# Attention and two expert layers on one core: two heads' products on halves of the TensorE array, and a scale taken from x1 itself

## The chip, the core and the metric

The kernel runs on one core of a Trainium2 chip, in one launch. The metric is the device time of that launch in microseconds (us); the kernel before takes 1054.92 us, the median of three runs (1052.87 to 1056.31).

## The reference, cut to what matters

Three stages follow one another. First an attention over 2 batches of 8 heads, 576 positions, 64 wide, which adds two results: a global one on positions averaged in fours, and a local one in which a position sees only neighbours less than 4 away.

```python
q_d, k_d, v_d = (a.reshape(B, H, 144, 4, 64).mean(axis=3) for a in (q, k, v))
out_up = np.repeat(sm_attn(q_d, k_d, v_d), 4, axis=2)       # softmax(q k^T / 8) v
mask = np.abs(pos[:, None] - pos[None, :]) < 4
attn = softmax(np.where(mask, q @ k^T / 8, -1e9))
x1 = out_up + attn @ v                                      # -> [1152 tokens, 512]
act = silu(x1 @ w_gate) * (x1 @ w_val)                      # 512 -> 1536
x2 = act @ w_out                                            # 1536 -> 512
P = eight rounds of row and column normalising of exp(x2 @ w_gate2)
out = sum over 8 experts e of P[:, e] * (relu(x2 @ w1[e]) @ w2[e])   # 512 -> 1024 -> 512
```

## The kernel before, in words

**Attention** (`attention`, lines 332 to 480). The 16 heads are worked as 8 pairs; a pair's two heads of 64 lie on the 128 partitions, the first on partitions 0 to 63. `load_pair` (287) loads k of a pair as one transfer and q as two, each head into its own half of a zeroed tile `qz` (288 KB in all for q): column block j holds head j on its 64 partitions and zeros on the others. So the product of `qz` block j with the whole k tile is head j's score, contracted over all 128 rows of the array. `scores(h)` (360) writes one head: a mask product, five windows of 128x128 positions (lines 366 to 372), and two products of the pooled q and k (line 374), into two of six PSUM banks (`bank`, tag "att"). VectorE takes the maxima, ScalarE the exponentials with their sums, GpSimd divides by the sums. `turn(h)` (404) transposes the weights on TensorE and ScalarE copies them back, again through two of the six banks. `combine(pr)` (421) multiplies them with v: `vz` and `vdz` hold v of each head beside 64 zero columns, so that the two heads' products, each 128 columns of weights wide, accumulate in the same PSUM columns (lines 430 and 438, 8 and 20 matmul instructions a pair, each f32 product being two). The result x1 of a pair, 128 features by 576 tokens, is scaled and split into two f16 parts `xhl` at once (line 450).

**Order of the pieces.** Each generator step is one piece in program order: the scores of 4 heads ahead (`AHEAD`), then turn(h), scores(h+4), and after each odd h combine. Tile pools hand out buffers, and a planner that follows program order as priority and its own cost model sets the order on each engine; that order is fixed in the program. All loads go through SP's one queue in program order: two `load_pair`, two `load_v` (two transfers for `vz`, one for `v4` each), then `load_va`, eight loads of a copy of v, 288 KB each, in four buffers. The next pair's loads wait for the buffers of the pair two back.

**The scale of x1.** x1 is bounded ahead of the attention from v: `x1_scale` (314) multiplies v by itself on TensorE (40 bf16 matmuls, line 322), takes the largest entry and makes a power of two of it (`pow2`), one for all of x1. The loads of `va` serve this alone.

**After it.** `gv_step` multiplies `xhl` with the gate and value weights, chunk 0 (tokens 0 to 511) in 24 matmuls of 512 columns for each of 12 weight tiles f, chunk 1 (tokens 512 to 1151) in 48 of 320, three f later (`LAG`). The first three f of chunk 0 (`NX`) use PSUM left over beside the attention, the others banks that the attention gives back at its end. The weights come as 64-bit floats: `prep_gv` (200) and `prep_wo` (214) convert, scale and split them, mostly on VectorE and ScalarE, in f order; two are placed in the attention's program (`PREP_AT`), others run beside it where there is room. From about 270 us on the two-layer experts follow, with no part in the change.

Of the kernel before, what the change touches and what calls it, by code (L numbers as in the profile page):

```python
# [7 lines left out]
F32 = mybir.dt.float32  # L8
# [31 lines left out]
AHEAD = 4  # L40
# [15 lines left out]
def tile_kernel(ctx, tc, qT, kT, vw, vd4, va, wgv, wo, wg2, w1, w2, out):  # L56
# [25 lines left out]
    qz = [ap.tile([P, 2, S], F32, tag=f"qz{i}", bufs=1, name=f"qz{i}") for i in range(2)]  # L82
    vz = [ap.tile([P, NW, 2, P], F32, tag=f"vz{i}", bufs=1, name=f"vz{i}") for i in range(2)]
    vdz = [ap.tile([HS, 2, 2, P], F32, tag=f"vdz{i}", bufs=1, name=f"vdz{i}") for i in range(2)]
# [12 lines left out]
    for i in range(2):  # L97
        G.memset(vz[i][:, :, 0, 64:], 0.0)
        G.memset(vz[i][:, :, 1, :64], 0.0)
        G.memset(vdz[i][:, :, 0, 64:], 0.0)  # L100
        G.memset(vdz[i][:, :, 1, :64], 0.0)
# [185 lines left out]
    def load_pair(pr):  # L287
        k = ap.tile([P, S], F32, tag="k", name=f"k{pr}")
        nc.sync.dma_start(k, kT[pr])
        q = qz[pr % 2]  # L290
        nc.sync.dma_start(q[:64, 0], qT[pr, :64])
        nc.sync.dma_start(q[64:, 1], qT[pr, 64:])
        ld[pr] = k

    v4s = {}

    def load_v(pr):
        v = vz[pr % 2]
        for j in range(2):
            nc.sync.dma_start(v[:, :, j, 64 * j:64 * j + 64], vw[pr, :, :, 64 * j:64 * j + 64])  # L300
        v4 = ap.tile([HS, 2, FAC, P], F32, tag="v4", bufs=1, name=f"v4{pr}")
        nc.sync.dma_start(v4, vd4[pr])
        v4s[pr] = v4

    vas = []
    x1s = []

    def load_va():
        for i in range(B * NPAIR):
            t = mp.tile([P, 2 * CH[1][1]], F32, tag="xT", bufs=4, name=f"va{i}")[:, :S]  # L310
            nc.sync.dma_start(t, va[i])
            vas.append(t)

    def x1_scale():


        ps = psg.tile([P, 512], F32, tag="y", name="vv")[:, :P]
        for i, t in enumerate(vas):
            b = t.bitcast(BF16)[:, 1::2]
            for lo in (0, P, 2 * P, 4 * P, 3 * P):  # L320
                n = min(P, S - lo)
                T.matmul(ps[:n, :n], lhsT=b[:, lo:lo + n], rhs=b[:, lo:lo + n],
                         start=(i, lo) == (0, 0), stop=(i, lo) == (B * NPAIR - 1, 3 * P))
        mx = tmp(1, "mxv")
        V.tensor_reduce(mx, ps, axis=AX.X, op=ALU.max)
        m = tmp(1, "mv")
        V.tensor_scalar(m.bitcast(U32), allmax(mx, 1, "v", True).bitcast(U32), 0x7F800000, 1, op0=ALU.bitwise_and,
                        op1=ALU.logical_shift_right)
        V.tensor_scalar(m.bitcast(U32), m.bitcast(U32), float(127 << 22), None, op0=ALU.add)
        x1s.extend(pow2(m, 1, "x1", room=4.0))  # L330

    def attention():
# [4 lines left out]
        qd, kd, exs, ats = {}, {}, {}, {}  # L337

        def pooled(pr):
            q, k = qz[pr % 2], ld[pr]  # L340
            qd[pr] = ap.tile([P, 2, SD], F32, tag="qd", name=f"qd{pr}")
            kd[pr] = ap.tile([P, SD], F32, tag="kd", name=f"kd{pr}")
            V.tensor_reduce(kd[pr], k.rearrange("p (s a) -> p s a", a=FAC), axis=AX.X, op=ALU.add)
            if pr not in QDV:
                t = ap.tile([P, 2, 2 * SD], F32, tag="qt", bufs=1, name=f"qt{pr}")
                G.tensor_tensor(t, q[:, :, 0::2], q[:, :, 1::2], op=ALU.add)
                G.tensor_tensor(qd[pr], t[:, :, 0::2], t[:, :, 1::2], op=ALU.add)
            else:
                V.tensor_reduce(qd[pr], q.rearrange("p j (s a) -> p j s a", a=FAC), axis=AX.X, op=ALU.add)

        def pooled_v(pr):
            v4, vd = v4s[pr], vdz[pr % 2]
            vt = ap.tile([HS, 2, 2, P], F32, tag="vt", bufs=1, name=f"vt{pr}")
            G.tensor_tensor(vt[:, 0], v4[:, :, 0], v4[:, :, 1], op=ALU.add)
            G.tensor_tensor(vt[:, 1], v4[:, :, 2], v4[:, :, 3], op=ALU.add)
            for j in range(2):
                h = slice(64 * j, 64 * j + 64)
                G.tensor_tensor(vd[:, :, j, h], vt[:, 0, :, h], vt[:, 1, :, h], op=ALU.add)

        def scores(h):  # L360
            pr, j = h // 2, h % 2
            q, k = qz[pr % 2], ld[pr]
            nm = f"{h}"
            ps = bank(f"s{nm}")
            T.matmul(ps[0], lhsT=identb, rhs=maskb.rearrange("p u w -> p (u w)"), start=True, stop=False)
            for w in range(NW - 1):
                ws = slice(WSTART[w], WSTART[w] + P)
                T.matmul(ps[0][:, w * P:(w + 1) * P], lhsT=q[:, j, ws], rhs=k[:, ws],  # L368
                         start=False, stop=w == NW - 2)
            T.matmul(ps[1][:, DW:DW + P], lhsT=identb, rhs=maskb[:, 0], start=True, stop=False)  # L370
            ws = slice(WSTART[4], WSTART[4] + P)
            T.matmul(ps[1][:, DW:DW + P], lhsT=q[:, j, ws], rhs=k[:, ws], start=False, stop=True)
            for t in range(2):
                T.matmul(ps[1][:HS, t * SD:(t + 1) * SD], lhsT=qd[pr][:, j, t * HS:(t + 1) * HS],
                         rhs=kd[pr], start=True, stop=True)
# [45 lines left out]
        def combine(pr):  # L421
            nm = f"{pr}"
            v, vd = vz[pr % 2], vdz[pr % 2]
            ps = bank(f"o{nm}")
            base = WCUT[3]
            nr = S - base
            n = 0
            for j in range(2):
                for c in range(2):
                    T.matmul(ps[1][:, nr:nr + SD], lhsT=vd[:, c, j], rhs=ats[2 * pr + j][:HS, 1, c * SD:(c + 1) * SD],  # L430
                             start=n == 0, stop=n == 3)
                    n += 1
            for w in range(NW):
                lo, hi = WCUT[w], WCUT[w + 1]
                dst = ps[0][:, lo:hi] if w < 3 else ps[1][:, lo - base:hi - base]
                off = (w * P if w < 4 else DW) + lo - WSTART[w]
                for j in range(2):
# [10 lines left out]
            b, k = pr // NPAIR, pr % NPAIR  # L448
            o = slice(b * S, (b + 1) * S)
            split(xhl[:, 0, k, o], xhl[:, 1, k, o], x1, x1s[0])  # L450

        NH = 2 * NPAIR * B

        def start(h):
            if h < NH:
                if h % 2 == 0:
                    pooled(h // 2)
                scores(h)
                if h % 2 and h // 2 + 2 < NPAIR * B:
                    load_pair(h // 2 + 2)  # L460

        for h in range(AHEAD):
            start(h)
            if h == 1:
                pooled_v(0)
                x1_scale()
            yield
        for h in range(NH):
            turn(h)
            yield  # L470
            start(h + AHEAD)
            yield
            if h % 2:
                pr = h // 2
                combine(pr)
                if pr + 2 < NPAIR * B:
                    load_v(pr + 2)
                if pr + 1 < NPAIR * B:
                    pooled_v(pr + 1)
# [7 lines left out]
    def gv_step(c, f, early):  # L487
# [4 lines left out]
        with tc.high_priority():  # L492
            V.tensor_scalar(iv[:, 0:1], gv_inv[f], x1s[1], 0.5 if early else 1.0, op0=ALU.mult, op1=ALU.mult)
# [138 lines left out]
    load_va()  # L632
# [150 lines left out]
_INS = ("qT", "kT", "vw", "vd4", "va", "wgv", "wo", "wg2", "w1", "w2")  # L783
# [38 lines left out]
```

## Time and profile before

| what | value |
|---|---|
| median of the runs | 1054.92 us (1052.87 to 1056.31) |
| the profiled execution | 1055.02 us, span 1053.2 us |
| TensorE (PE) busy | 1019.6 us, 97% |
| VectorE (DVE) busy | 767.7 us, 73% |
| ScalarE (ACT) busy | 450.1 us, 43% |
| GpSimd (POOL) busy | 94.3 us, 9% |
| read from HBM | 64.50 MB |

All later times are counted in the span of the profiled execution; 1.8 us lie around it. PE stands for TensorE's matmuls and PEld for its weight loads, which overlap them; SPq is SyncE's queue, which issues the transfers. L368 is line 368 of the kernel. An f32 product appears as two matmul instructions. The duration that a row gives for one matmul runs to the modelled end of its pipeline; the pace of a row of matmuls is read from the chain of waits, which gives starts. "PEclk" is the clock that was granted to TensorE, 1.00 being 2.4 GHz and 0.5 the lower level of 1.2 GHz; values between are mixtures over a stretch.

### The profile page before, as it was taken

To read this page: it belongs to the slowest core of one execution; us is meant where nothing else is said; L and a number is where in the kernel's file an instruction comes from. 1 tells how busy PE (TensorE), PEld (TensorE's weight loads), DVE (VectorE), ACT (ScalarE), POOL (GpSimd) and SP (SyncE) were. 2 spreads that over 40 slices of the span, in tenths; PEclk is the share of its full clock that TensorE was granted. 3 is DMA by queue.
4 is the path that set the end of the run, shared out by engine and by line. 5 is a ranking of instruction groups with operands and counts; after the bars stand their busy time and mean duration, and the time that the engine had idled before them with its cause. 6 is when DMAs were issued, how large, how long until landed. Compare 5 with 4: busy or idle time off the path is not lost.

```text
span 1053.2 us, 16460 instructions
## 1 busy us (share of the span) xinstructions
PE 1019.6 (97%) x6520; PEld 655.2 (62%) x6521; DVE 767.7 (73%) x1578; ACT 450.1 (43%) x931; POOL 94.3 (9%) x138
## 2 busy tenths in 40 slices
PE   6787998999999999999999999999999999999998
PEld 4676754656567866665756756666575675666644
DVE  7888559887681899878759749758875974984631
ACT  3586656756460656345215414414521541441200
POOL 4786100000000200000000000000000000000000
PEclk9899899999999999999999999999999999999999
DMA  9652132432020022112112100301211110020011
GB/s 263 189 146 52 56 118 85 156 121 81 1 81 1 2 81 80 42 40 81 41 40 79 43 16 26 120 1 41 80 41 40 76 46 17 24 81 1 1 41 51
DMA packets 23614, 67.93 MB, mean 64 GB/s; under 512 B 12208, under 2 KB 12464, under 8 KB 17136
## 3 DMA queue, kind: packets, MB, share of 16 engines
q1 hardware_dynamic: 23536, 66.87, 19.1%
q8 instruction: 51, 0.84, 0.3%
q14 instruction: 27, 0.22, 0.1%
HBM read 64.50 MB, written 2.36 MB: 63 GB/s over the span
## 4 chain that ended last, share of the span: by engine, by line
PE 86%; DVE 6%; ACT 3%; DMA 2%; issue 2%; SPq 0%; POOL 0%; ACTq 0%; DVEq 0%
PE y L172 35%; PE p L172 30%; PE gv L172 8%; PE wo L172 7%; DMA k<-in_kT 2%; PE o L438 2%; ACT ex L386 1%; PE o L430 1%; DVE cvg L196 1%; PE s L368 1%; PE lgps L556 1%; DVE cvg L191 1%; DVE cvg L195 0%; PE t L410 0%; DVE act L528 0%
## 5 line engine op out<-in xcount | busy, mean ns | idle before, releaser
L172 PE MATMUL y<-w,hhl 128*128 128x512 f16 (+1 forms) x1752 | 396.2, 376 | 0.0
L172 PE MATMUL p<-bop,w 128*128 128x320 f16 (+1 forms) x2688 | 354.6, 286 | 0.8 <-DVE u L693 0.7
L172 PEld LDWEIGHTS <-w 128*128 128x128 f16 x2688 | 263.0, 98 | 90.8 <-issue 1.5
L172 PEld LDWEIGHTS <-hhl 128*128 128x128 f16 x1752 | 171.4, 98 | 178.2
L721 ACT ACTIVATE hhl<-h 128x640 f16<-128x640 f32 (+1 forms) x128 | 83.3, 676 | 160.6 <-DVE h L693 160.5
L172 PE MATMUL gv<-xhl,gv 128*128 128x320 f16 (+1 forms) x864 | 145.5, 328 | 6.5 <-ACT gv L164 4.1
L172 PEld LDWEIGHTS <-gv 128*128 128x128 f16 x864 | 84.2, 98 | 62.8 <-issue 5.6
L752 DVE SCALAR_TENSOR_TENSOR acc<-y,pe,acc 128x512 f32<-128x512 f32 (+1 forms) x64 | 47.3, 740 | 101.3 <-PE y L172 100.5
L164 ACT ACTIVATE w<-r,s_w 128x256 f16<-128x256 f32 (+1 forms) x96 | 71.1, 783 | 115.2 <-PE y L172 86.3
L722 DVE SCALAR_TENSOR_TENSOR hhl<-h,hhl 128x640 f16<-128x640 f32 (+1 forms) x128 | 94.6, 754 | 15.2 <-ACT hhl L721 13.7
L693 DVE SCALAR_TENSOR_TENSOR h<-p,u 128x256 f32<-128x256 f32 (+1 forms) x192 | 85.2, 453 | 19.9 <-PE p L172 14.0
L165 DVE SCALAR_TENSOR_TENSOR w<-r,s_w,w 128x256 f16<-128x256 f32 (+1 forms) x96 | 78.2, 834 | 16.8 <-ACT w L164 16.7
L172 PE MATMUL wo<-ahl,wo 128*128 128x320 f16 (+1 forms) x432 | 71.5, 326 | 0.0
L693 DVE SCALAR_TENSOR_TENSOR u<-p,u 128x320 f32<-128x320 f32 (+1 forms) x128 | 57.5, 449 | 4.3 <-PE p L172 3.2
L164 ACT ACTIVATE w<-cmb,s_w 128x512 f16<-128x512 f32 x64 | 43.0, 710 | 40.5 <-DVE cmb L253 37.9
L172 PEld LDWEIGHTS <-wo 128*128 128x128 f16 x432 | 42.3, 99 | 26.9
L151 POOL PARTITION_ALL_REDUCE g_w<-gm_w x16 | 5.9, 372 | 569.1 <-DVE gm_w L147 563.2
L710 ACT ACTIVATE s<-p 128x256 f32<-128x256 f32 (+1 forms) x64 | 25.4, 397 | 56.5 <-PE p L172 56.4
L141 DVE TENSOR_REDUCE mxw<-r 128x1 f32<-128x1024 f32 x32 | 37.5, 1213 | 12.6 <-DMA r<-in_w 12.6
L165 DVE SCALAR_TENSOR_TENSOR w<-cmb,s_w,w 128x512 f16<-128x512 f32 x64 | 46.2, 743 | 0.0
L273 ACT ACTIVATE j<-r 128x1024 f16<-128x1024 f32 x32 | 33.4, 1045 | 26.0 <-DMA r<-in_w 26.0
L693 DVE SCALAR_TENSOR_TENSOR u<-p,s 128x256 f32<-128x256 f32 (+1 forms) x64 | 28.8, 451 | 5.2 <-PE p L172 3.9
(201 smaller groups left out, 952.4 us busy)
## 6 DMA issues: line engine op xcount, KB each, us to landing
r<-in_w SPq DMA_DIRECT2D x32, 1024.0 KB, 5.4
rawg<-in_wgv SPq DMA_DIRECT2D x12, 1024.0 KB, 6.4
rawo<-in_wo SPq DMA_DIRECT2D x6, 1024.0 KB, 4.8
vz<-in_vw SPq DMA_DIRECT2D x16, 160.0 KB, 3.4
k<-in_kT SPq DMA_DIRECT2D x8, 288.0 KB, 6.5
qz<-in_qT SPq DMA_DIRECT2D x16, 144.0 KB, 4.4
v<-in_vd SPq DMA_DIRECT2D x8, 288.0 KB
va<-in_va SPq DMA_DIRECT2D x8, 288.0 KB, 7.7
```

The lines of the kernel that those rows point to most:

```text
L141: V.tensor_reduce(o, i, axis=axis, op=ALU.max, apply_absolute_value=True)
L164: return (A.activation(hi, src, AF.Copy, scale=s), V.scalar_tensor_tensor(lo, src, s, hi, op0=ALU.mult, op1=ALU.subtract))
L165: V.scalar_tensor_tensor(lo, src, s, hi, op0=ALU.mult, op1=ALU.subtract))
L172: T.matmul(ps, lhsT=wf(i, k), rhs=xf(j, k), start=n == 0, stop=n == 3 * nk - 1)
L191: V.scalar_tensor_tensor(f, h, HI_MIN, f, op0=ALU.max, op1=ALU.max)
L273: A.activation(junk, t[:, 2 * j:2 * j + 2].rearrange("p a n -> p (a n)"), AF.Abs, accum_out=mx[:, 2 * i + j:2 * i + j + 1])
L438: T.matmul(dst, lhsT=v[:, w, j], rhs=ats[2 * pr + j][:, w // 4, off:off + hi - lo], start=j == 0, stop=j == 1)
L693: V.scalar_tensor_tensor(o, ps, HSC, u, op0=ALU.mult, op1=ALU.add)
L710: A.activation(s1, p1, AF.Copy, scale=HSC)
L721: ra = A.activation(t[:, 0], h, AF.Relu)
L722: rv = V.scalar_tensor_tensor(t[:, 1], h, 0.0, t[:, 0], op0=ALU.max, op1=ALU.subtract)
L752: V.scalar_tensor_tensor(acc[t][:, ds], ps, p[:, t:t + 1], acc[t][:, ds], op0=ALU.mult, op1=ALU.add)
```

## The change

q, v and the pooled forms are kept without zeros, one tile with a head on each half. A score product uses the 64 partitions of its head for both operands, and the two heads' products of a pair are issued alternately; in `combine` each head uses 64 columns of weights and writes its own 64 PSUM partitions, alternately as well. The scores of a pair are one piece now, into four of the six banks. q, and v, come as one transfer each. The zero fills, `load_va` and `x1_scale` are gone; instead the magnitudes of each x1 are taken, and the splitting waits for the last pair of a batch: `x1_split(0)` splits the first 512 tokens by the largest of pairs 0 to 3 and copies the last 64 aside, `x1_split(1)` splits the rest by the largest of all eight. `gv_step` uses the inverse scale of its chunk.

```diff
-    for i in range(2):
-        G.memset(qz[i][64:, 0], 0.0)
-        G.memset(qz[i][:64, 1], 0.0)
...
-        q = qz[pr % 2]
-        nc.sync.dma_start(q[:64, 0], qT[pr, :64])
-        nc.sync.dma_start(q[64:, 1], qT[pr, 64:])
+        q = ap.tile([P, S], F32, tag="q", name=f"q{pr}")
+        nc.sync.dma_start(q, qT[pr])
...
+        v_s[pr] = ap.tile([P, NW, P], F32, tag="v", name=f"v{pr}")
+        nc.sync.dma_start(v_s[pr], vw[pr])
...
-    def x1_scale():
-        ps = psg.tile([P, 512], F32, tag="y", name="vv")[:, :P]
-        for i, t in enumerate(vas):
...
+    def x1_split(b, x1):
+        mx = x1mx[:, :(b + 1) * NPAIR]
+        s, x1i[b] = pow2(allmax(mx, (b + 1) * NPAIR, f"x1{b}", True), 1, f"x1{b}")
+        n = CH[1][0] if b == 0 else S
+        if b:
+            o = slice(CH[1][0], S)
+            split(xhl[:, 0, :, o], xhl[:, 1, :, o], tail, s)
+        for k, t in enumerate(x1):
+            o = slice(b * S, b * S + n)
+            split(xhl[:, 0, k, o], xhl[:, 1, k, o], t[:, :n], s)
+            if b == 0:
+                A.copy(tail[:, k], t[:, n:])
...
+        def scores(pr):
+            q, k = ld[pr]
+            pss = [bank(f"s{2 * pr + j}") for j in range(2)]
+            hj = [slice(64 * j, 64 * j + 64) for j in range(2)]
...
+            for w in range(NW):
+                ws = slice(WSTART[w], WSTART[w] + P)
+                for ps, h in zip(pss, hj):
+                    dst = ps[0][:, w * P:(w + 1) * P] if w < 4 else ps[1][:, DW:DW + P]
+                    T.matmul(dst, lhsT=q[h, ws], rhs=k[h, ws], start=False, stop=w >= NW - 2)
+            for t in range(2):
+                for ps, h in zip(pss, hj):
+                    T.matmul(ps[1][:HS, t * SD:(t + 1) * SD], lhsT=qd[pr][h, t * HS:(t + 1) * HS],
+                             rhs=kd[pr][h], start=True, stop=True)
             for j in range(2):
+                weights(2 * pr + j, pss[j])
...
+            for c in range(2):
+                for j, h in enumerate(hj):
+                    T.matmul(ps[1][h, nr:nr + SD], lhsT=vd[:, c, h], rhs=ats[2 * pr + j][:HS, 1, c * SD:(c + 1) * SD],
+                             start=c == 0, stop=c == 1)
...
-                    T.matmul(dst, lhsT=v[:, w, j], rhs=ats[2 * pr + j][:, w // 4, off:off + hi - lo],
-                             start=j == 0, stop=j == 1)
+                for j, h in enumerate(hj):
+                    T.matmul(dst[h], lhsT=v[:, w, h], rhs=ats[2 * pr + j][:, w // 4, off:off + hi - lo],
+                             start=True, stop=True)
...
-            split(xhl[:, 0, k, o], xhl[:, 1, k, o], x1, x1s[0])
+            absmax(x1mx[:, pr:pr + 1], x1)
+            x1t.append(x1)
+            if len(x1t) == NPAIR:
+                x1_split(pr // NPAIR, x1t)
+                x1t.clear()
...
+        for pr in range(2):
+            start(pr)
...
+        for pr in range(NP):
+            for h in (2 * pr, 2 * pr + 1):
+                turn(h)
+                yield
+            start(pr + 2)
             yield
+            combine(pr)
```

## Rows read from the trace of the kernel before

**Rows 1.** From the page: busy time, share of the span and instructions of each engine.
```profile
PE 1019.6 (97%) x6520; PEld 655.2 (62%) x6521; DVE 767.7 (73%) x1578; ACT 450.1 (43%) x931; POOL 94.3 (9%) x138
```

**Rows 2.** Busy time by stretch (start:end, length, busy us and instructions of each engine, granted clock, busy share of the DMA engines, GB/s): up to the first x1, the rest of the attention, the gate-and-value stage in two parts, and the experts.
```profile
0.00:47.00 47.00, 31.38 (x200) 26.14 (x202) 36.94 (x90) 22.23 (x97) 27.26 (x45) 0.89 0.86 242
47.00:129.00 82.00, 73.77 (x547) 63.63 (x546) 62.05 (x146) 59.25 (x216) 49.37 (x63) 0.94 0.32 87
129.00:180.00 51.00, 45.54 (x255) 24.71 (x254) 37.16 (x69) 28.91 (x46) 0.73 (x2) 0.97 0.28 104
180.00:270.00 90.00, 89.82 (x577) 56.36 (x576) 73.49 (x134) 58.93 (x106) 3.23 (x6) 1.00 0.30 106
...
400.00:1053.00 653.00, 649.92 (x4057) 396.81 (x4055) 460.67 (x923) 220.47 (x372) 4.55 (x13) 1.00 0.13 46
```

**Rows 3.** VectorE on the timeline, the x1 of a pair: the first of the eight and the last (start, duration of both instructions).
```profile
46.97 0.81 DVE L444 TENSOR_TENSOR x<-o,avd 128x364 f32<-128x364 f32 x2
...
128.61 0.82 DVE L444 TENSOR_TENSOR x<-o,avd 128x364 f32<-128x364 f32 x2
```

**Rows 4.** The chain of work that ended last, in order of time (start, us, what), from 16 to 47 us.
```profile
16.54 9.17 DMA k<-in_kT
25.77 9.62 DMA k<-in_kT
...
35.56 0.52 issue
36.09 1.15 DVE nb L380
...
38.89 1.33 PE o L430 x4
40.22 0.51 PE sm_v L157 x2
40.73 2.85 PE o L438 x12
43.58 0.97 PE o L430 x4
44.55 1.65 PE o L438 x8
```

**Rows 5.** The DMA view of the first 40 us: packets and bytes, and the queue's share of the 16 engines' time.
```profile
DMA packets 6185, 10.29 MB, mean 257 GB/s; under 512 B 3225, under 2 KB 3225, under 8 KB 5798
...
q1 hardware_dynamic: 6182, 10.26, 93.2%
```

**Rows 6.** The line that loads k, over the whole run: its transfers' time from issue to landing.
```profile
DMA to landing us min/median/max: 3.1/6.5/9.6
```

**Rows 7.** The timeline of the first 11 us: what VectorE does ahead of the identity matrix, and TensorE's first scores behind it.
```profile
1.24 3.77 DVE L109 TENSOR_SCALAR dist<-dist 128x1 f32<-128x1 f32 x5
...
5.69 1.35 DVE L349 TENSOR_REDUCE qd<-qz 128x288 f32<-128x1152 f32 x1
...
7.65 0.75 DVE L343 TENSOR_REDUCE kd<-k 128x144 f32<-128x576 f32 x1
...
10.09 0.23 DVE L117 TENSOR_SCALAR identb<-dist 128x128 bf16<-128x128 f32 x1
...
10.71 0.59 PE L365 MATMUL s<-maskb,identb 128*128 128x512 bf16 x1 [7.22 <-DMA vz<-in_vw]
```

**Rows 8.** The chain again, at the full clock, from which the pace of each kind of matmul is read (us for xcount of them, one head or one pair).
```profile
71.06 0.25 PE t L414 x4
71.31 0.22 PE s L365
71.53 0.89 PE s L368 x8
72.48 0.28 PE s L372 x2
72.75 0.49 PE s L374 x4
73.24 0.44 PE t L410 x4
...
80.23 0.49 PE o L430 x4
80.72 0.86 PE o L438 x8
...
127.26 5.18 PE gv L172 x24
```

**Rows 9.** TensorE's first products of v with itself on the timeline (start, duration of all).
```profile
16.84 2.11 PE L322 MATMUL vv<-va 128*128 128x128 bf16 x20
```

**Rows 10.** Groups by line and form over 0 to 135 us (busy us, mean ns of one, idle before): the score matmuls, and the weight loads of the products of v with itself.
```profile
L368 PE MATMUL s<-k,qz 128*128 128x128 f32 x128 | 18.1, 286 | 0.7 <-DMA k<-in_kT 0.6
...
L322 PEld LDWEIGHTS <-va 128*128 128x128 bf16 x32 | 2.3, 98 | 1.0 <-DMA va<-in_va 0.6
```

**Rows 11.** Whom TensorE waited for in the first 130 us (us in total, times, longest).
```profile
PE o L430 <- ACT ex L386: 9.5, 3, 4.7
```

**Rows 12.** ScalarE on the timeline, one head's exponentials from the first to the copies behind the last.
```profile
63.06 0.37 ACT L386 ACTIVATE ex<-s,nb 128x128 f32<-128x128 f32 x1 [0.31 <-DVE nb L383]
...
65.49 0.59 ACT L416 COPY at<-t 128x512 f32<-128x512 f32 x1
```

**Rows 13.** Busy time in stretches of 10 us (columns as in rows 2): where the granted clock fell.
```profile
30.00:40.00 10.00, 5.11 (x37) 3.97 (x36) 7.90 (x18) 3.84 (x19) 5.34 (x6) 0.80 0.90 237
40.00:50.00 10.00, 10.00 (x62) 9.45 (x62) 9.27 (x21) 6.49 (x27) 10.00 (x14) 0.69 0.47 148
```

More of the change, by code (lines that the diff above doesn't have):

```diff
@@ L95, in tile_kernel @@
         V.memset(sts[i], 1.0)
[L97 to L101, printed above, removed]
+    x1mx = cp.tile([P, B * NPAIR], F32, name="x1mx")
+    tail = ap.tile([P, KD, S - CH[1][0]], F32, tag="tail", bufs=1, name="tail")
     ones = cp.tile([P, P], F32, name="ones")
@@ L305, in tile_kernel @@
[L305 to L312, printed above, removed]
-    def x1_scale():
-        ps = psg.tile([P, 512], F32, tag="y", name="vv")[:, :P]
-        for i, t in enumerate(vas):
[L319 to L330, printed above, removed]
+        q = ap.tile([P, S], F32, tag="q", name=f"q{pr}")
@@ L355, in pooled_v @@
             G.tensor_tensor(vt[:, 1], v4[:, :, 2], v4[:, :, 3], op=ALU.add)
-            for j in range(2):
[L357 to L362, printed above, removed]
-            nm = f"{h}"
[L364 to L375, printed above, removed]
+            G.tensor_tensor(vds[pr], vt[:, 0], vt[:, 1], op=ALU.add)
@@ new lines, in scores @@
+        def scores(pr):
+            q, k = ld[pr]
+            pss = [bank(f"s{2 * pr + j}") for j in range(2)]
+            hj = [slice(64 * j, 64 * j + 64) for j in range(2)]
+            for ps in pss:
+                T.matmul(ps[0], lhsT=identb, rhs=maskb.rearrange("p u w -> p (u w)"), start=True, stop=False)
+            for ps in pss:
+                T.matmul(ps[1][:, DW:DW + P], lhsT=identb, rhs=maskb[:, 0], start=True, stop=False)
+            for w in range(NW):
[7 more added lines that the diff above has]
+                             rhs=kd[pr][h], start=True, stop=True)
+            for j in range(2):
+                weights(2 * pr + j, pss[j])
@@ L376, in scores, with weights @@
+        def weights(h, ps):
+            nm = f"{h}"
             mx, sm = stm[h % 2], sts[h % 2]
@@ L426, in combine @@
             nr = S - base
[L427 to L432, printed above, removed]
+            hj = [slice(64 * j, 64 * j + 64) for j in range(2)]
+            for c in range(2):
+                for j, h in enumerate(hj):
+                    T.matmul(ps[1][h, nr:nr + SD], lhsT=vd[:, c, h], rhs=ats[2 * pr + j][:HS, 1, c * SD:(c + 1) * SD],
+                             start=c == 0, stop=c == 1)
             for w in range(NW):
@@ L447, in combine, with start @@
                                 op=ALU.add)
-            b, k = pr // NPAIR, pr % NPAIR
-            o = slice(b * S, (b + 1) * S)
-            split(xhl[:, 0, k, o], xhl[:, 1, k, o], x1, x1s[0])
[L452 to L464, printed above, removed]
+            absmax(x1mx[:, pr:pr + 1], x1)
[3 more added lines that the diff above has]
+                x1t.clear()
+        NP = NPAIR * B
+        def start(pr):
+            if pr < NP:
+                pooled(pr)
+                scores(pr)
+                if pr + 2 < NP:
+                    load_pair(pr + 2)
+        for pr in range(2):
+            start(pr)
+            if pr == 0:
                 pooled_v(0)
-                x1_scale()
             yield
-        for h in range(NH):
-            turn(h)
             yield
-            start(h + AHEAD)
-            yield
[L473 to L479, printed above, removed]
+        for pr in range(NP):
[3 more added lines that the diff above has]
+            start(pr + 2)
+            yield
+            combine(pr)
+            if pr + 2 < NP:
+                load_v(pr + 2)
+            if pr + 1 < NP:
+                pooled_v(pr + 1)
+            yield
+            yield
             yield
```

45 lines of the change are left out of this document (18 added, 27 removed).

## The prediction

> **What bounds the kernel now.** I read the page first: TensorE is busy for 97% of the span [rows 1], so whatever does not give TensorE less work, or less waiting, gives nothing. The table by stretch says where waiting is left [rows 2]: from 180 us on there is none (89.8 of 90 us, 649.9 of 653), up to 47 us there are 15.6 us of it, in the rest of the attention 8.2, and up to 180 us 5.5. The change touches the attention, so it can win in the first 129 us and must hand on what it wins to the gate-and-value stage, which is in step with TensorE only as long as its weights are converted in time.
>
> The eight x1 give the pace of the attention [rows 3]: the first at 46.97, the last at 128.61, so 11.66 us a pair behind a long start. The chain of waits explains the start [rows 4]: from 16.5 to 35.4 it is nothing but two loads of k, 9.17 and 9.62 us each, then VectorE, then the first combine at 38.9, which had waited for its bank [rows 11]. These loads are late because the queue is full: in the first 40 us the transfers take 93.2% of the 16 engines' time for 10.26 MB, 257 GB/s [rows 5], while the quickest load of k landed in 3.1 us [rows 6]. In the second part, from 47 to 129 us, TensorE is the tightest engine, 73.8 of 82 us; VectorE has 62.1, ScalarE 59.3, GpSimd 49.4 [rows 2].
>
> **The change, part by part.**
>
> *Loads.* `load_va` took 8 x 288 KB = 2.36 MB out of the one queue, all issued before 24 us: at 257 GB/s [rows 5] 9.2 us of a queue on which the chain waits for 18.8 us [rows 4]. Each of the two loads of k stands behind about half of it, so I expect them to land in about 4.6 and 5.0 us. Merging the halves of q and of v takes SP issues away, two a pair, of which none stands in the chain behind 16 us; I put it at nothing. Bounds: 9.2 us if the chain ends at the queue, 0 if VectorE (36.9 of 47 us busy) takes its place. I take 8, nearer to the chain's row than to VectorE's, because that engine idles for 10 us here. Behind the loads VectorE's maxima are late next.
>
> *VectorE at the start.* The identity matrix, for which the first score really waits (it is written at 10.09, the score starts at 10.71), stands in VectorE's queue behind two reductions of `qz` over 1152 columns, 1.35 us each; over 576 one takes 0.75 [rows 7]. That is 1.2 us. The five small operations that take 3.77 us beside GpSimd's zero fills [rows 7] may lose some 2 us as those go; I count 0 and keep the 2 as a bound. Together the first pair comes about 9 us earlier (0 to 13).
>
> *TensorE's work per pair.* At the full clock one head's scores take 0.22 for the mask, 0.89 and 0.28 for ten window matmuls, 0.06 for the small mask between them, 0.49 for the pooled ones; one turn 0.44 + 0.11 + 0.25; a combine 2 x 0.49 + 20 x 0.1075 = 3.1 [rows 8]. A pair is 2 x 1.94 + 2 x 0.80 + 3.1 = 8.6 us. On two halves the pooled products fall from 0.98 to 0.49 and the combine from 3.1 to 1.6, if the halves run beside each other. The windows (2.34 a pair) are open between no gain and half: the products of v with itself, 128 columns of weights against 128 moving columns in bf16, come every 2.11 / 20 = 0.105 us [rows 9], though 512 moving columns take 0.216 (5.18 / 24) [rows 8] and so 128 about 0.054; their loads take 98 ns each [rows 10]. So a load of 128 columns paces its matmul, and the windows keep 128 columns of weights for each head. The combine has 64 and escapes this. By this row the windows stay at 2.34, and a pair costs 0.56 + 2.34 + 0.49 + 1.6 + 1.6 = 6.6 us; if the loads of the two halves overlapped, the windows would take 1.17 and a pair 5.4. I take 6.6, as the row has it. The Trainium skill says in TensorEngine Tiling (Key Properties) that different tiles load weights and multiply in parallel, which would be the 5.4; no row of this kernel shows two tiles at work. Either way 2.0 to 3.2 us a pair go, 16 to 26 in all, and `x1_scale` takes 40 x 0.105 = 4.2 with it. The sum hardly hangs on which, since TensorE is not the tightest engine then.
>
> *What is late next.* Without those matmuls VectorE is the tightest. It gains the magnitudes of x1, 128 x 576 each, as the reduction of k: 0.75 us a pair [rows 7]; so (62.1 + 7 x 0.75) / 7 = 9.6 us a pair at 100%. TensorE as the tightest engine reached 90% of this stretch; at 92% VectorE gives 10.4 us a pair. The other candidate is the loop through the PSUM banks: a pair's scores now hold four of six banks until both heads' exponentials are done. That is 2.2 to 3.4 us of scores, about 1 us of VectorE, and twice 65.49 - 63.06 = 2.43 us of ScalarE [rows 12], 8.1 to 9.3 us: just under VectorE's. I take 10.4: 7 x (11.66 - 10.4) = 9 us. Bounds: 9.0 a pair, where conversions of weights now done beside the attention slide out behind it (+19), and 13.5, the loop at a slow clock (-13, below).
>
> *The scale.* `x1_split(0)` comes after pair 3, and the chunk 0 products can't start on pairs 0 to 2 any more. Behind it stand three f of chunk 0, 24 matmuls of 0.216 us each, 15.5 us together [rows 8], and four more pairs of at least 9 us to hide them beside: nothing. `x1_split(1)` puts a maximum, two small matmuls and five splits (about 6 us, an estimate from 0.75 us operations) ahead of chunk 1; TensorE has the last early f and f = 3 of chunk 0 for that time, 10 us. Nothing, if the weights of f = 3 are there. On TensorE's queue the two small matmuls of the maximum wait for VectorE with scores behind them: 1 us each time. The 64 columns copied aside are off the path. What is not free is the conversion of weights: TensorE already lost 5.5 us between 129 and 180 us, with VectorE at 37.2 of 51 us [rows 2], and an attention that ends sooner leaves less done. I count 2 us for all of it, 0 to 8.
>
> **Sum.** 9 + 9 - 2 = 16 us, from the profiled execution's 1055.0 us, which is the median of the runs (1054.9): **1039 us**. As a check, 20 to 30 us of TensorE's work go, so its idle time would grow by 4 to 14 us, which is what a second engine at 92% makes of the attention.
>
> **The rivals.**
>
> *VectorE lets go.* The planner puts attention first and conversions into the gaps, so they slide into the later stage, where VectorE has 73.5 of 90 us [rows 2]. Pace 9.0: 9 + 18.6 - 1 = 27, so 1028 us. For it: that slack. Against: between 129 and 180 us the slack is not on time. 0.17.
>
> *The halves don't run beside each other.* The change would then not do what it says, TensorE keeps 8.6 us a pair and 11.66 stays: 9 - 2 = 7, so 1048 us. For it: weight loads that pace (above). Against: the combine's loads are halved in columns. A change of the array's shape might also cost a drained pipeline: a score matmul's row lasts 286 ns [rows 10] where its pace is 0.111, so 0.175 us, four times a pair, 5.6 us in all and 1053. The Trainium skill's TensorEngine Tiling (Key Properties) has this rule, that switching the tiling mode drains the engine; no row here shows it or its price. 0.15.
>
> *Slower: the bank loop at the lower clock.* As TensorE does less it waits more, and the clock falls: after 10 us with 4.9 idle, the granted clock in the next 10 was 0.69, a mixture of the 2.4 and 1.2 GHz levels [rows 13]. At 1.2 GHz the scores of a pair take 4.4 to 6.8, and with them the loop 10.3 to 12.7; one conversion of 1.2 us ahead of the maxima on VectorE makes it 13.5. Then 7 x 1.84 = 13 us lost, 9 won, 2 lost: 1061 us. It decides above 12.7 us a pair. For it: four banks of six in one piece, and the first combine's wait for a bank now [rows 11]. Against: the chunk 0 products keep TensorE occupied from pair 4 on. 0.10.
>
> **How the numbers follow.** The forecast has 0.58, with its own range 1030 to 1047 (first pair 0 to 13 us earlier, pace 9.9 to 11). Faster or slower by 0.3%, 3.2 us, is about what a measurement can tell. Faster: the forecast less 0.03, the first rival, and two thirds of the second: 0.55 + 0.17 + 0.10 = 0.82 less 0.02 for mixtures = 0.80. Same: 0.08, from the second rival with its drains and the forecast's tail. Slower: 0.10 and 0.02 of the second rival. The range takes in the first rival, with some room for a quicker start, and the second up to its drains, and leaves the slower one out: 1021 to 1052.
>
> **What would show it.** Right: loads of k landing in about 5 us ahead of 30 us; the first x1 at 38, the last near 111, VectorE 90% busy between; the combine's matmuls at half their pace. Wrong: a first x1 later than 45 (the queue was not the bound), a pace of 11.5 or more with TensorE under 70% busy (banks or clock), window matmuls at 0.055 (loads do overlap), or a wait for weights of more than 10 us behind the attention.

## The result, and the profile after

The change made the kernel slower: **1068.01 us** (median of 4 runs, 1067.53 to 1069.93) against 1055.15 (4 runs of the kernel before beside them, 1052.87 to 1056.31), a ratio of **1.0140, 95% interval 1.0121 to 1.0158**. The forecast was 1039 us, range 1021 to 1052: the sign was wrong. The profiled execution took 1069.93 us, its span is 1068.1 (before: 1053.2).

The page first. TensorE is busy for 4.1 us less than in [rows 1], and the span is 14.9 longer, so it stands idle for 52.6 us instead of 33.6.
```profile
PE 1015.5 (95%) x6485; PEld 636.1 (60%) x6485; DVE 767.2 (72%) x1591; ACT 451.5 (42%) x936; POOL 80.7 (8%) x118
```
The table by stretch, with the columns and the stretches of [rows 2]:
```profile
0.00:47.00 47.00, 22.03 (x154) 15.16 (x155) 32.19 (x81) 21.70 (x81) 21.49 (x30) 0.78 0.60 192
47.00:129.00 82.00, 69.27 (x520) 52.08 (x520) 58.40 (x155) 57.45 (x232) 41.07 (x58) 0.83 0.24 74
129.00:180.00 51.00, 45.29 (x242) 23.63 (x243) 33.34 (x60) 24.05 (x40) 0.00 (x0) 0.94 0.23 83
180.00:270.00 90.00, 85.65 (x533) 52.13 (x531) 76.81 (x143) 58.77 (x105) 4.16 (x7) 0.98 0.35 129
400.00:1053.00 653.00, 652.12 (x4063) 397.04 (x4061) 471.66 (x949) 224.16 (x378) 5.19 (x14) 1.00 0.12 46
```
The experts are unchanged (652.1 of 653). In the first 129 us TensorE is busy for 13.9 us less (105.2 before, 91.3 now), and this is not time won: part of those products only moved behind the attention, and there is more waiting, at a lower granted clock, 0.78 and 0.83 instead of 0.89 and 0.94.

The first and the last x1, as in [rows 3]:
```profile
53.14 0.77 DVE L427 TENSOR_TENSOR x<-o,avd 128x364 f32<-128x364 f32 x2
...
114.68 0.82 DVE L427 TENSOR_TENSOR x<-o,avd 128x364 f32<-128x364 f32 x2 [2.16 <-ACT avd L424]
```
So the attention starts 6.2 us later and then runs at 8.8 us a pair instead of 11.66, and it ends 13.9 us earlier. What comes behind it gives that back twice over. This is the chain of waits from the last x1 on (start, us, what):
```profile
114.68 0.83 DVE x L427 x2
...
117.67 0.31 PE sm_gv L145 x2
117.98 4.38 PE gv L162 x12
...
122.92 2.77 PE gv L162 x12
125.72 0.74 DVE act L502
126.47 1.14 DVE cvg L181
...
130.88 1.16 ACT gv L196 x2
...
132.67 4.06 PE gv L162 x12
...
146.84 2.71 PE gv L162 x12
...
280.90 13.38 PE wo L162 x62
```
Three rows of TensorE's timeline beside it, with the wait ahead of a row and what ended it in brackets:
```profile
132.08 0.59 PE L145 MATMUL sm_gv<-ident,mxg 128*1 128x128 f32 x2 [6.41 <-ACT gv L196]
...
139.65 5.56 PE L162 MATMUL gv<-xhl,gv 128*128 128x512 f16 x25
...
146.47 0.38 PE L145 MATMUL sm_gv<-ident,mxg 128*1 128x128 f32 x2 [1.25 <-ACT gv L196]
```
and the chain of the kernel before at the same two places:
```profile
132.75 2.71 PE gv L172 x12
...
267.05 12.73 PE wo L172 x59
```
`x12` are the twelve products of one half of a step of `gv_step`. In chunk 0 the step f = 0 starts at 117.98 and f = 1 at 132.67; f = 2 follows f = 1 directly, from 139.9 on (the row of 25 is the last product of f = 1 and the 24 of f = 2), and f = 3 starts at 146.84. In the kernel before, f = 0 ran beside the attention (its first product at 73.92), f = 1 in the gaps of the last pairs, f = 2 around the last x1 (127.26, [rows 8]), and f = 3 began at 132.75, 4.1 us behind the last x1; here it begins 32.2 us behind it. **The sum**: start +6.2, seven pairs -20.1, from the last x1 to f = 3 of chunk 0 +28.0, together +14.1. From there the two traces run in step: the first product with `wo` comes at 267.05 before and at 280.90 after, +13.9; the span +14.9.

What the 32.2 us hold, by the chain and the timeline: 3.0 us for the second scale (up to 117.67); 19.2 us of products of f = 0, 1 and 2, of which 15.5 are their pace at the full clock [rows 8] and some 2.9 the lower clock (the first halves of f = 0 and f = 1 take 4.38 and 4.06 us at a granted clock of 0.62 and 0.67, the second halves 2.77 and 2.76); 7.7 us in which TensorE waits (6.41 and 1.25); and 2.4 us of small matmuls and the short waits behind them. The kernel before had 3.8 us of products and one small matmul there. So more than half of the 28.0 us are products that are no longer hidden beside the attention, and about a quarter is waiting.

Why TensorE waits. Behind f = 0 the chain is VectorE's conversion of the weights of f = 3 (`cvg`, L181 to L187), ScalarE's magnitudes (`gv` L196), and then `sm_gv`, a matmul of one column for the maximum, which stands in TensorE's queue *ahead* of the products of f = 1. Those had their weights since the attention, but they start only behind it. The conversion of f = 3 in its turn is issued only behind the last operation of f = 0 (`act` L502): `moe1_step` ties `prep_gv(f + 2)` to `gv_done[0, f - 1]`. So f = 0, the conversion and maximum of f = 3, and f = 1 follow one another with nothing beside them, 6.41 us of waiting. For f = 4 the same order costs only 1.25 us, because the products of f = 2 run beside its conversion. In stretches of 10 us neither engine is full:
```profile
110.00:120.00 10.00, 7.35 (x57) 5.06 (x56) 5.30 (x15) 4.93 (x12) 0.00 (x0) 0.84 0.00 0
120.00:130.00 10.00, 5.42 (x21) 2.17 (x19) 9.58 (x18) 5.04 (x8) 0.00 (x0) 0.84 0.00 0
130.00:140.00 10.00, 7.67 (x29) 3.17 (x30) 3.98 (x11) 2.98 (x4) 0.00 (x0) 0.73 0.31 107
140.00:150.00 10.00, 8.60 (x41) 3.72 (x39) 5.52 (x8) 3.34 (x6) 0.00 (x0) 1.00 0.30 105
```
VectorE, said to be the tightest engine, has 24.4 of these 40 us.

Why none of these products ran beside the attention: `x1_split(0)` needs the maximum over pairs 0 to 3. Pair 3's x1 is there at 85.07, the two small matmuls of the scale stand at 90.08 and 92.72, the last split ends at 100.65, 14 us ahead of the last x1; and in TensorE's queue the planner put all that is left of the attention, and the second scale too, ahead of the first product.

**The start.** The queue did get free, and k lands quickly, as forecast (answering [rows 5] and [rows 6]: 8.41 MB instead of 10.26, and the line of the loads of k):
```profile
q1 hardware_dynamic: 2496, 8.41, 65.2%
```
```profile
DMA to landing us min/median/max: 2.6/2.8/4.2
```
But the first pair's division, without which its `turn` can't start, comes at 27.46 instead of 19.28. The timeline of after, with the releaser in brackets:
```profile
13.72 1.15 ACT L183 ACTIVATE cvg<-rawg 128x1024 f32<-128x1024 f32 x1 [11.72 <-DMA rawg<-in_wgv]
14.90 0.69 DVE L184 TENSOR_SCALAR cvg<-cvg 128x1024 f32<-128x1024 f32 x1 [1.82 <-ACT cvg L183]
...
17.75 1.14 ACT L183 ACTIVATE cvg<-rawg 128x1024 f32<-128x1024 f32 x1
...
27.46 1.04 POOL L381 TENSOR_TENSOR ex<-ex,rs 128x512 f32<-128x512 f32 x1
```
and of before:
```profile
19.28 1.04 POOL L397 TENSOR_TENSOR ex<-ex,rs 128x512 f32<-128x512 f32 x1 [4.07 <-DVE nb L380]
20.70 1.15 ACT L193 ACTIVATE cvg<-rawg 128x1024 f32<-128x1024 f32 x1
```
With `load_va` gone, the first gate weights are issued at 3.91 us instead of 9.86, and their conversion begins at 13.72 instead of 20.70: it now lies *ahead of and between* the first two heads' exponentials, on ScalarE and VectorE. GpSimd has the pooled sums of v (`pooled_v`) of pairs 1 and 2 ahead of that division as well, and the latter wait for their load until 25.67; before it had pair 0's alone there. From 20 to 40 us TensorE is busy for 9.15 us, at a granted clock of 0.50, all at the 1.2 GHz level (before: 12.83 us, at 0.90). What the conversions, GpSimd's order and the clock each cost here was tried for GpSimd's order alone (e9).

### The profile page after: what moved, and what is told of

The parts are those of the page before. It is cut to its first block, busy times and chain, and to the rows that moved or that the text cites. A ratio compares the mean times of both kernels' runs of the same rounds, so it can differ in the third digit from the quotient of the medians.

```text
span 1068.1 us, 16322 instructions
## 1 busy us (share of the span) xinstructions
PE 1015.5 (95%) x6485; PEld 636.1 (60%) x6485; DVE 767.2 (72%) x1591; ACT 451.5 (42%) x936; POOL 80.7 (8%) x118
## 4 chain that ended last, share of the span: by engine, by line
PE 83%; DVE 8%; DMA 3%; ACT 3%; issue 1%; POOL 1%; SPq 0%; ACTq 0%; POOLq 0%; DVEq 0%
PE y L162 33%; PE p L162 28%; PE gv L162 11%; PE wo L162 7%; DMA v<-in_vd 2%; DMA r<-in_w 1%; PE s L350 1%; DVE w L155 1%; DVE cvg L186 1%; DVE cvg L187 1%; PE lgps L541 1%; PE o L421 1%; ACT gv L196 1%; PE t L394 1%; DVE gv L155 0%
## 5 line engine op out<-in xcount | busy, mean ns | idle before, releaser
L706 DVE SCALAR_TENSOR_TENSOR hhl<-h,hhl 128x640 f16<-128x640 f32 (+1 forms) x128 | 94.5, 753 | 15.2 <-ACT hhl L705 13.8
L677 DVE SCALAR_TENSOR_TENSOR h<-p,u 128x256 f32<-128x256 f32 (+1 forms) x192 | 85.1, 453 | 20.1 <-PE p L162 14.8
L131 DVE TENSOR_REDUCE mxw<-r 128x1 f32<-128x1024 f32 x32 | 37.5, 1213 | 14.1 <-DMA r<-in_w 14.1
L677 DVE SCALAR_TENSOR_TENSOR u<-p,s 128x256 f32<-128x256 f32 (+1 forms) x64 | 28.8, 450 | 6.7 <-PE p L162 3.9
```

Of the source, the lines that this page charges most:

```text
L131: V.tensor_reduce(o, i, axis=axis, op=ALU.max, apply_absolute_value=True)
L677: V.scalar_tensor_tensor(o, ps, HSC, u, op0=ALU.mult, op1=ALU.add)
L706: rv = V.scalar_tensor_tensor(t[:, 1], h, 0.0, t[:, 0], op0=ALU.max, op1=ALU.subtract)
```

## The experiments

Every kernel was run beside the kernel before on the same chip, and the ratio is to that. In the expectations the letters stand for: A, the scale's barrier sets the loss; A2, the conversions of weights bound the stage behind the attention; B, the halves themselves cost; C, the clock; C2, the banks or VectorE set the pace; D, GpSimd's order sets the start. What they call the start of f = 3 (162.47 in the trace after) is, by the order of TensorE's queue, the second half of f = 4 of chunk 0; the first product with `wo` serves here instead.

| kernel | median us | ratio (95%) | first x1 | last x1 | first `wo` |
|---|---|---|---|---|---|
| before | 1052.7 to 1055.2 | 1 | 46.97 | 128.61 | 267.05 |
| after | 1068.01 | 1.0140 (1.0121 to 1.0158) | 53.14 | 114.68 | 280.90 |
| e1 halves alone | 1058.94 | 1.0051 (1.0033 to 1.0068) | 47.64 | 128.72 | 272.57 |
| e2 scale alone | 1068.39 | 1.0139 (1.0119 to 1.0158) | 50.65 | 113.62 | 281.98 |
| e3 steps in the attention | 1065.10 | 1.0110 (1.0090 to 1.0130) | 52.61 | 115.77 | 278.37 |
| e4 heads in turn | 1071.41 | 1.0166 (1.0144 to 1.0189) | 47.36 | 116.43 | 285.06 |
| e5 maxima on GpSimd | 1051.98 | 0.9983 (0.9963 to 1.0002) | 51.97 | 113.46 | 263.68 |
| e6 tie removed | 1067.09 | 1.0130 (1.0112 to 1.0149) | 52.39 | 120.18 | 278.97 |
| e7 as e5, on before | 1056.12 | 1.0028 (1.0013 to 1.0044) | 47.38 | 143.84 | 270.21 |
| e8 as e1, with filling matmuls | 1053.19 | 0.9994 (0.9979 to 1.0009) | 46.67 | 122.42 | 264.86 |
| e9 sums of v behind divisions | 1064.53 | 1.0092 (1.0057 to 1.0126) | 48.52 | 111.30 | 277.41 |
| e10 = e5 + e9 | 1047.47 | 0.9956 (0.9939 to 0.9972) | 48.51 | 108.17 | 258.04 |
| e11 = e10 + filling | 1046.65 | 0.9932 (0.9910 to 0.9953) | 42.94 | 109.53 | 259.71 |
| e12 = e11 + in turn | 1051.40 | 0.9994 (0.9983 to 1.0004) | 41.26 | 110.41 | 261.91 |

### One part of the change at a time: e1 and e2

e1 has the halves and the old scale (`load_va`, `x1_scale`, splits pair by pair); e2 the zero-padded products and the new scale.

> The halves alone: products without zeros as in the changed kernel, but x1 is scaled from v's own products and split after each pair, as before. Theory A (the splitting that waits for four pairs pushes the gate-and-value products of chunk 0 behind the attention, where each waits for its weights): those products are back beside the attention, 1038 to 1056 us. Theory B (the halves themselves cost: scores that run one head after the other, a late start, the clock at 1.2 GHz): 1064 us or more, as the changed kernel.

> The new scale alone: zero-padded products as before, but the magnitudes of x1 and the splitting that waits for the batch, without the loads and products of v with itself. Theory A: the first chunk 0 product comes after the last combine again and the time is 1066 to 1080 us. Theory B: 1045 to 1056 us, the earlier loads being a gain and nothing else lost.

e2 is the whole loss, 1.0139 against the change's 1.0140. And its attention ends at 113.62, as early as with the halves: the quicker pace is not the halves' work. It fits that products and conversions are no longer done beside the attention; e2 does not separate these from the products of v that are gone. e1 lies between its two ranges: the halves alone leave the last x1 where it was (128.72 to 128.61) and cost half a per cent, with the old scale.

### Where the steps stand, and what stands ahead of them: e3, e5, e6, e7

e3 writes the first three steps into the attention's program:
```diff
+GV_AT = (27, 33, 39)
     for n, _ in enumerate(attention()):
         if n in PREP_AT:
             prep_gv(PREP_AT.index(n))
+        if n in GV_AT:
+            moe1_step(GV_AT.index(n))
```


> The changed kernel with the first three steps of the gate-and-value stage written into the attention's program, from pair 4 on, so that the planner places them there. Theory A: chunk 0 products start near 97 us, the fourth step near 148 us in place of 162, total 1050 to 1058 us. Theory B: 1063 us or more, since nothing of the start or of the scores changes.

A miss, for the most part: 3 us of 14. f = 0 did go beside the attention (its first product at 97.90) and f = 3 began at 129.61, 17 us earlier. But now the conversions and the second scale's splits came late (the splits of batch 1 at 146.54 in its chain), and the products of chunk 1 waited for those until 147.72.

e5 takes the maxima of f = 3 to 5 off TensorE; GpSimd does them, as for the later f. e7 does the same to the kernel before.
```diff
-NSHORT = 6
+NSHORT = 3
```


> The changed kernel with the largest weight magnitude of the tiles f = 3 to 5 taken by GpSimd, as for the later tiles, in place of two small matmuls on TensorE. Theory A (behind the attention each chunk 0 step stands on TensorE's queue behind the small matmul of weights three f later, which wait for the step before: 14.4 us a step): the steps f = 1 and 2 follow at once, f = 3 starts near 140 us in place of 162, total 1046 to 1056 us. Rival A2 (the conversions themselves are the bound, wherever their maximum is taken): 1064 us or more.

> The kernel before with the same edit (GpSimd takes the maximum of f = 3 to 5). Theory A: the steps stand beside the attention there and little waits on them, so 1050 to 1058 us, within 4 us of the kernel before. If it gains as much as the changed kernel with this edit does, the wait is no matter of the change.

One number brings the time back to that of the kernel before, 1068 to 1052, with the scale's barrier, the late products and the tie all in place; in the kernel before it costs 3 us. TensorE's timeline of e5, and its stretches of 10 us that answer to those of after:
```profile
121.70 7.93 PE L162 MATMUL gv<-xhl,gv 128*128 128x512 f16 x36 [0.25 <-DVE u_gv L124]
...
130.57 6.33 PE L162 MATMUL gv<-xhl,gv 128*128 128x512 f16 x28 [0.94 <-DVE act L501]
```
```profile
110.00:120.00 10.00, 7.35 (x52) 4.46 (x52) 6.23 (x17) 5.87 (x13) 0.00 (x0) 0.84 0.00 0
120.00:130.00 10.00, 9.38 (x42) 4.15 (x41) 9.61 (x18) 4.56 (x8) 0.00 (x0) 0.97 0.00 0
130.00:140.00 10.00, 8.09 (x37) 3.37 (x37) 9.77 (x21) 6.59 (x12) 1.34 (x2) 1.00 0.56 202
140.00:150.00 10.00, 9.67 (x63) 6.04 (x62) 9.39 (x13) 5.76 (x8) 0.00 (x0) 1.00 0.27 100
```
Between 120 and 150 VectorE has 28.8 of 30 us (19.1 in after) and TensorE 27.1 (21.7). Nothing was made quicker; conversions and products overlap again. f = 1 follows f = 0 without a gap (the row of 36), and in this stretch VectorE is now near its limit, which it was not in after.

But the three maxima are not the whole loss. In e5 f = 3 begins at 135.9 (the row of 28 is f = 2 and its first four), 22.5 us behind the last x1 instead of 32.2: of the 28.0 us 9.7 go, and 18.3 stay. The first `wo` comes 17.2 us earlier than in after, and 6.3 of these lie behind f = 3, where the change had lost nothing: from f = 3 to the first `wo` it is 134.3 us before, 134.1 in after and 127.8 in e5. Nor is e7 a clean counterpart. From f = 3 (144.43) to `wo` it wins as well, 125.8 us instead of 134.3; but its last x1 comes 15 us later, and the chain there goes through GpSimd's maxima of f = 3 and 4 (`g_gv`, at 115.23 and 133.17), which now stand in the attention, with 4.5 and 5.8 us ahead of them in which the engine waits for nothing that the profile shows. So e5 shows that the waiting can be taken out, and how much the time gains; it does not show that the waiting was all that the change lost.

e6 keeps the maxima on TensorE and takes the tie away (`prep_gv(f + np_)` without its `issue_after`).

> The change with the tie between prep_gv(f+2) and the last operation of step f of chunk 0 taken away; the maxima of f = 3 to 5 stay on TensorE. If the tie itself keeps the weights of f = 3 back, f = 3 starts near 140 us and the time is as with the maxima on GpSimd, 1052. If it is the place of the small matmul of the maximum in TensorE's queue, which the planner still lays behind the products of the early steps, little moves: 1064 to 1068.

1067.09: taking the tie away alone wins next to nothing. Without it f = 3's conversion moved into the attention, which ended 5.5 us later for it. The steps f = 0, 1 and 2 start at 123.4, 132.7 and 140.1, and f = 3 at 145.7, 25.5 us behind the last x1 instead of 32.2, so of the 6.7 us won there 5.5 were lost in the attention. And the next small matmul of a maximum, still ahead of its products, came only 2.5 us earlier (165.22 in after), and the way to the next long row of products behind it is nearly as long as in after (168.9 to 190.2 there):
```profile
143.15 19.57 PE gv L162 x108
162.73 0.31 PE sm_gv L145 x2
163.04 3.38 PE gv L162 x24
...
186.36 92.62 PE gv L162 x576
```

### What the halves do on TensorE: e4 and e8

In after the two heads' window products stand in turn for the first three pairs; for the five behind them the planner had put one head's behind the other's. TensorE's timeline of after, at a granted clock of 1.00: the windows of pair 1, in turn, then those of the last pair, and the combine of another:
```profile
13.67 1.16 PE L350 MATMUL s<-k,q 64*128 64x128 f32 x16
...
94.12 1.16 PE L350 MATMUL s<-k,q 64*128 64x128 f32 x8
95.21 0.39 PE L343 MATMUL s<-maskb,identb 128*128 128x512 bf16 x1
95.53 1.16 PE L350 MATMUL s<-k,q 64*128 64x128 f32 x8
...
98.75 0.71 PE L414 MATMUL o<-at,vd 72*64 72x144 f32 x8
99.29 1.16 PE L421 MATMUL o<-at,v 128*64 128x120 f32 x20
100.38 0.66 PE L394 MATMUL t<-ident,ex 128*128 128x128 f32 x4
```
In turn, sixteen of both heads take 1.16 us; one head behind the other, eight take as long. From start to start those eight take 95.21 - 94.12 = 1.09 us, 0.136 each against 0.111 on the padded array [rows 8]. The same half is not slower: from the second to the eighth they follow one another every 0.11 us (94.33 to 95.01). What is dearer is going from the mask product, on all rows, to a half and back: from the mask to the first window 0.32 us instead of 0.22 (95.21 to 95.53), from the first to the second 0.21 instead of 0.11, from the eighth to the next mask 0.20 instead of 0.11. This happens four times a pair, and the scores of this pair take 98.75 - 93.81 = 4.94 us, 1.06 more than the 3.88 (2 x 1.94) of the prediction's padded sum. The combine, whose halves do alternate, takes 100.38 - 98.75 = 1.63 a pair instead of 3.1. e4 forces the score matmuls of a pair into the written order, head by head in turn:
```diff
+            last = []
+            def mm(*args, **kw):
+                with tc.issue_after(last[-1].ins) if last else nullcontext():
+                    last.append(T.matmul(*args, **kw))
...
-                    T.matmul(dst, lhsT=q[h, ws], rhs=k[h, ws], start=False, stop=w >= NW - 2)
+                    mm(dst, lhsT=q[h, ws], rhs=k[h, ws], start=False, stop=w >= NW - 2)
```


> The changed kernel with the score products of a pair held in alternating order of the heads, where the planner had put one head's behind the other's. The window products should go from 0.135 us each to 0.07 or less if the halves run beside each other, and stay at 0.105 or more if their weight loads of 128 columns pace them. Theory A: the total stays within 3 us of 1068, the wait for the fourth step's weights being untouched. Theory B: 1054 to 1062 us.

The halves do run beside each other. The same pair in e4, in a stretch (98 to 101 us) whose granted clock was 0.50, the 1.2 GHz level:
```profile
98.24 2.51 PE L346 MATMUL s<-k,q 64*128 64x128 f32 x20
100.53 1.17 PE L346 MATMUL s<-kd,qd 64*72 64x144 f32 x8
```
Twenty window matmuls in 100.53 - 98.24 = 2.29 us, 0.1145 each at half the clock, where 0.111 is the padded pace at the full one. But the kernel got slower still (1071.41), a little outside both ranges, and TensorE ran longer at the lower clock. Summed over 5 us stretches of the first 130 us, from the granted clock of each (1.00 counted as all at 2.4 GHz, 0.50 as all at 1.2), the time at the lower level is 20.6 us before, 49.1 after, 57.9 in e1 and 58.1 in e4. That TensorE has less to do there is the likely reason; e4 alone does not show it.

e8 asks what that costs: e1, and four matmuls of 512 columns on zeros behind each head's transposes.
```diff
+        def fill(nm):
+            py = psg.tile([P, 512], F32, tag="y", name=f"fill{nm}")
+            for _ in range(4):
+                T.matmul(py, lhsT=warm[:, :P], rhs=warm, start=True, stop=True)
...
                 turn(h)
+                fill(h)
                 yield
```


> The halves alone with the old scale, and behind the transposes of each head four full-array bf16 matmuls of 512 columns on zeros that nothing reads, 0.86 us a head at the full clock. Theory C (the clock: with less to do TensorE runs 58 of the first 130 us at 1.2 GHz, before 21): time at 1.2 GHz falls under 35 us, the last x1 comes 3 us or more earlier than 128.7, total 1048 to 1056 us. Rival C2 (banks, VectorE and ScalarE set the pace at either clock): the last x1 at 127 us or later and the total 1057 us or more.

Useless work made it faster, 1058.94 to 1053.19, and the last x1 came at 122.42 instead of 128.72. From 40 to 80 us, e1:
```profile
40.00:60.00 20.00, 18.43 (x143) 14.21 (x141) 15.02 (x41) 15.02 (x60) 12.74 (x19) 0.76 0.44 136
60.00:80.00 20.00, 19.79 (x113) 14.44 (x114) 13.45 (x40) 12.45 (x49) 11.33 (x15) 0.68 0.36 115
```
and e8:
```profile
40.00:60.00 20.00, 19.74 (x165) 13.47 (x165) 18.12 (x47) 17.10 (x67) 14.04 (x20) 1.00 0.38 118
60.00:80.00 20.00, 19.95 (x177) 13.95 (x176) 12.95 (x33) 14.99 (x65) 14.03 (x20) 1.00 0.47 151
```
TensorE counts as busy for 18 to 20 of 20 us in both; at 0.68 to 0.76 it gets through 256 matmuls, at 1.00 through 290 and 52 filling ones besides. So with the old scale the halves' gain was there and, as far as these two runs show, the clock took it back; the filling also adds to what the planner orders, and that was not held fixed.

### The start, and versions that go further: e9 to e12

e9 lets GpSimd do the pooled sums of a pair's v only behind the divisions of the pair ahead (`pooled_v(pr + 1)` issued behind the last division of pair `pr`).

> The changed kernel with GpSimd's pooling of the next pair's v held behind the division of the pair before, where the planner had put the pooling of pairs 1 and 2 ahead of the first division, waiting for their loads. Theory D (that order makes the first x1 late): the first x1 at 46 us or earlier in place of 53.1, the last x1 3 us or more earlier, total 1060 to 1065 us. Rival (the clock or VectorE makes it late): first x1 at 51 us or later, total within 2 us of 1068.

The first x1 came 4.6 us earlier (48.52), the last 3.4 and the first `wo` 3.5. The first division itself moved by only 1 us (26.41): ahead of it the chain of e9 shows the conversions on VectorE. What those cost was not tried. The time is in the range of D, the first x1 2.5 us later than it asked.

> The change with the maxima of f = 3 to 5 on GpSimd and with the pooled sums of v behind the divisions. Each alone took 16 and 3.5 us from 1068. If they act on different stretches (the stage behind the attention, the first 50 us) they add: 1048. If what the attention wins is given back before f = 3 because the chain there is x1_split and three steps, the order of GpSimd's queue gives nothing more: 1052.

> The same with four matmuls of 512 columns on zeros behind each head's transposes, 16 heads. With the old scale these gave 5.7 us back (1058.9 to 1053.2), by the clock. If the clock is still what the attention lacks: last x1 2 to 6 us earlier than without them, 1043 to 1046. If the early steps of chunk 0 already keep TensorE occupied, or the 13.8 us of dummy work at full clock stand in its way: 1048 to 1054.

> The same as the one before, and the two heads' score matmuls in turn. In turn, a pass took 0.0755 us at a clock of 0.78 against 0.135 at 1.0 one head behind the other. With the dummy matmuls beside it, if TensorE's scores are on the path: 3 to 6 us less than with the fill alone, 1039 to 1043. If VectorE and the banks set the pace: no difference.

e10 adds the two: **1047.47, 0.9956 (0.9939 to 0.9972)**, 0.4% faster than the kernel before and 2% faster than the change. The filling, worth 5.7 us in e1, shows no difference here: e11's interval overlaps e10's, its first x1 is 5.6 us earlier and its last 1.4 later. With the heads in turn (e12) it is 4.8 us slower, which neither expectation had; both heads' scores then end together and VectorE's first maxima come later, but this was only argued. What sets the pace of the attention in e10 to e12 stays open, and so does what the halves are worth in e10, since the padded products were not run with its two edits.

## Why the prediction was wrong

*The scale, counted at 2 us (0 to 8)* is the step that failed. "Four more pairs of at least 9 us to hide them beside: nothing" took it for granted that products which could start at 100 us would; the planner put all three steps behind the attention. Measured: 28.0 us more from the last x1 to f = 3, some 15 of them the products themselves, 3 the second scale, 7.7 waiting. e2, with the new scale alone, has the whole loss. The conversions were named as "what is not free", but as work of VectorE; they cost by what stands ahead of the products in TensorE's queue: with three small matmuls gone from there (e5) 9.7 of the 28.0 us go, and without the tie alone (e6) 6.7, of which the attention gave back 5.5. The two small matmuls for which I charged 1 us were those of the scale; the dear ones are those of `prep_gv`, which nobody had changed.

*The loads, +8 us.* The first half held: k lands in 2.8 us (4.6 to 5.0 forecast). The step "behind the loads VectorE's maxima are late next" named the successor rightly and priced it at nothing: the same freed queue brought the gate weights 6 us earlier and their conversions ahead of the first softmax, and the first x1 came 6.2 us later instead of 9 earlier. GpSimd's order has 4.6 us of that (e9); that the conversions have a part in the rest is read from the trace, and was not tried. A first x1 later than 45 was my own sign for this step being wrong.

*TensorE's work per pair.* The combine is right (1.63 for 1.6). "A load of 128 columns paces its matmul, the windows stay at 2.34" is wrong where the heads take turns: 2.29 us at half the clock are about 1.15 at the full one, the 1.17 of the other bound. The Trainium skill's rule in TensorEngine Tiling (Key Properties), that different tiles load weights and multiply in parallel, agrees with e4. As built the windows gained nothing in five of the eight pairs, because the planner had not kept the turns, and the pooled products there stayed at 0.49 for four. The cost of changing the array's shape was left out of the sum and stood in a rival alone, at four times 0.175, 0.7 us a pair; with the heads one behind the other it measured 1.06. This agrees with the Trainium skill's rule in TensorEngine Tiling (Key Properties) that switching the tiling mode drains the engine.

*Pace 10.4 by VectorE, 9 us.* Measured 8.8, nearly the 9.0 of the rival "VectorE lets go", and by its mechanism: the work slid out. That rival gave back 1 us for it, by the slack that VectorE has from 180 us on. e2, at 9.0 us a pair, shows that it has little to do with the halves. Nor was VectorE the bound that the 10.4 took it for: between 47 and 129 us it is busy for 58.4 of 82 us, not 90%. What sets the 8.8 stays open.

*The slower rival* (the bank loop at the lower clock) had the sign and a part of the mechanism. The clock did fall, and e1 and e8 price that at 5.7 us without the new scale; but the pace never came near its 12.7 us a pair, and its place was not where the change lost. (Its loop, 12.7 and 1.2, is 13.9 us, not 13.5; this changes nothing here.)

## What to carry to other kernels

An instruction of one column can hold up a full engine: look at what stands *ahead* of the products in the queue, and whether it waits for something that only the products before release. Before counting work as hidden beside a stage, find who orders it there; when the earliest start of a piece moves, take the cost of its being put last as the bound. And a queue set free can bring forward every load in it, as the gate weights here: see which engine the earliest one sets to work, and what it delays.

## What was not expected of the hardware

The half that is worked alone keeps the padded array's pace (0.111 us for 128 moving columns in f32), so halves that don't alternate win nothing here, and each way from all rows to a half and back cost about 0.27 us (1.06 for four), so as the planner laid them they lost. Filling matmuls on zeros bought 5.7 us at a cost of 64 x 0.216 = 13.8 us of TensorE's time (the full-clock pace of 512 columns, [rows 8]), since the granted clock between 40 and 80 us rose from about 0.72 to 1.00.
